# Output projections of a recurrent attention layer: one 512-column matmul per head instead of four of 128, with an fp32 fold

## The chip, the core and the metric

The kernel runs on one core of a Trainium2 chip. The core has a matrix engine (PE, with its weight loads shown apart as PEld), a vector engine (DVE), a scalar engine (ACT), a general engine (POOL) and a queue engine (SP); 16 DMA engines move data between the chip's memory (HBM) and the on-chip memory. Matmul results land in PSUM, of which a tile of 128 partitions by 512 fp32 numbers fills one bank of eight. The metric is the device time of one execution, in microseconds.

## The reference, cut to what matters

The program is a forward and backward pass of one block: a recurrent attention over segments of 32 rows with 8 memory rows, and a gated feed-forward layer. What the change touches is the recurrence:

```python
# S = 2048 rows, D = 512, H = 32 heads of 128, M = 8 memory rows, 64 segments of 32 rows
mem = mem0
for s in range(64):
    h = concatenate([mem, x[s]])                # 40 rows
    q, k, v = h@Wq, h@Wk, h@Wv                  # per head
    o = softmax(mask(q k^T * scale)) v          # per head, 40 rows
    o = einsum('bhte,hed->btd', o, Wo)          # output projection: sum over 32 heads
    mem = o[:, :8]                              # the next segment needs these 8 rows
    outs.append(o[:, 8:])
```

The backward pass runs the segments in reverse. There the gradient of `h` is a sum over 96 products (32 heads of dV, dK and dQ with the transposed Wv, Wk and Wq), and its 8 memory rows feed the segment before.

## The kernel before

`phase2` is the forward recurrence, `phase4` the backward one; `phase3` lies between them (the feed-forward layer, forward and backward), `phase5` behind (weight gradients). In `phase2` and `phase4` a segment is one turn of a Python loop over 64; everything is unrolled. The code is recorded in that order, and a scheduling layer then fixes each engine's own row of instructions; within an engine that row is kept at run time. Data of all heads lie as 12 groups of 128 columns, three heads of 40 rows to a group; `pi` counts three parts of four groups (12, 12 and 8 heads).

One forward segment: `proj_bank` makes Q, K and V (384 matmuls of 128x128 weights by 40 columns, line 371), then scores, exponentials, sums, products with V and transposes. `fillers` are transposes left over from the segment before, put into gaps. `outproj` (line 446) then takes 32 rows of every head as weights (a tile of 128x32) and multiplies with the head's 512 columns of `Wo`. `col_mms` (line 198) does that in four matmuls of 128 columns, one in each column tile of the array (`tile_position`), so that column chunk `c` of the sum over heads grows in partitions 32c to 32c+31 of `at_ps`. `rows_to_mem` (line 204) copies nothing but a transpose: `at_sb` (ACT, line 491), the transpose `memtp` (PE, line 208), and the copy of its 8 memory columns into the next segment's `hT` (DVE, line 209). `store_a` writes `at_sb` to the DRAM tensor `AOA`.

The remaining 8 rows of each head are collected by `TailRows` (POOL copies, line 1339) over four segments; their projection runs in four pieces (`chunk`, line 1363) into `ao_tps`, one piece per following segment, and ends with a DVE copy `ao_tsb` (line 1377).

The backward segment has the same end: `dot_bank` (128 matmuls of 40 columns, line 1004), transposes, `ds_part`, `grad_part` (dV, dK, dQ), and between them `dht` (line 1046), which calls `col_mms` 96 times into `dh_ps`; then `dh_sb` (line 1084), `memtp`, `dyT` (the next segment's input), and the tail pieces `dh_tps` of 24 heads each. The first matmul of the next segment reads `hT` or `dyT`, so a segment's end and the next one's beginning are a chain.

The lines before, word for word:

```python
        for c in range(self.cfg.DC):
            self.nc.tensor.matmul(ps[32 * c:32 * c + 32, :], lhsT=lhsT, rhs=w[:, c * 128:(c + 1) * 128],
                                  start=start, stop=stop, tile_position=(0, 32 * c))
```

Of the kernel before, what the change touches and what calls it, by code (L numbers as in the profile page):

```python
# [7 lines left out]
BF16 = mybir.dt.bfloat16  # L8
F32 = mybir.dt.float32
AF = mybir.ActivationFunctionType  # L10
# [30 lines left out]
class K:  # L41
# [73 lines left out]
    def phase0(self):  # L115
# [2 lines left out]
        D, DC = cfg.D, cfg.DC  # L118
        self.ident = const.tile([128, 128], BF16, name="ident")
        make_identity(nc, self.ident[:])  # L120
        self.ones = const.tile([128, 128], BF16, name="ones")
        nc.vector.memset(self.ones[:], 1.0)
        L, M = cfg.L, cfg.M
# [71 lines left out]
                nc.sync.dma_start(self.MODROW[:, q * 768:(q + 1) * 768],  # L195
                                  modrow[32 * q:32 * q + 1, :, :].rearrange("p h n -> p (h n)"))

    def col_mms(self, ps, lhsT, w, start, stop):

        for c in range(self.cfg.DC):  # L200
            self.nc.tensor.matmul(ps[32 * c:32 * c + 32, :], lhsT=lhsT, rhs=w[:, c * 128:(c + 1) * 128],  # L201
                                  start=start, stop=stop, tile_position=(0, 32 * c))

    def rows_to_mem(self, psp, rows_sb, dst):

        nc, M = self.nc, self.cfg.M
        tp = psp.tile([128, self.cfg.DC, 32], BF16, name="memtp", tag="p")
        nc.tensor.transpose(tp[:, :, :].rearrange("p c r -> p (c r)"), rows_sb[:], self.ident[:])  # L208
        nc.vector.tensor_copy(dst[:, :, 0:M], tp[:, :, 0:M])  # L209

    def load_x_rows(self, dst, j, a, b):

# [65 lines left out]
    def phase2(self):  # L278
# [6 lines left out]
        with ExitStack() as ctx:  # L285
# [42 lines left out]
            Qsts = ptiles("Qst", 2, zero=False)  # L328
            Ksts = ptiles("Kst", 2, zero=False)

            p1_tile = self.phase1_setup(ctx, lambda: ps_b16("p1tp"))
            P1_AHEAD = 3
# [57 lines left out]
                    fillers.pop(0)()  # L390

            nseg_t = 128 // T
            tail = TailRows(self, sb2, psb, 1, "ao", self.AOA, self.AOB)
            for s in range(NS):
                i2 = s % 2
                if s % nseg_t == 0:
# [48 lines left out]

                def outproj(pi):
                    if at_ps[0] is None:
                        at_ps[0] = psp.tile([128, 128], F32, name="at_ps", tag="p")
                    for h in range(pi * PG * 3, min(H, (pi + 1) * PG * 3)):
                        off = (h // 3) * GW + (h % 3) * L  # L450
                        self.col_mms(at_ps[0], OT[:, off:off + 32], Wo[:, h, :], n_at[0] == 0, n_at[0] == H - 1)
                        n_at[0] += 1

                proj_bank("q", 0, QT, hT, "act")
# [36 lines left out]
                nc.scalar.activation(at_sb[:], at_ps[0][:], AF.Copy)  # L491
                tail.collect(s % nseg_t, [OT])
                tail.chunk()
                if hT_next is not None:
                    self.rows_to_mem(psp, at_sb, hT_next)
                tail.store_a(s, at_sb)
                if s % nseg_t == nseg_t - 1:
                    tail.begin(s - nseg_t + 1, [Wo])
                nc.gpsimd.dma_start(self.VT[s], gl3(VT))
# [2 lines left out]
                    filler()  # L502

                def mk_fillers(s=s, i2=i2, QT=QT, KT=KT, ET=ET, rden=rden):
                    Pst, Qst, Kst = Psts[i2], Qsts[i2], Ksts[i2]
# [396 lines left out]
    def phase4(self):  # L902
# [7 lines left out]
        with self.p4_ctx as ctx:  # L910
# [69 lines left out]
            nc.vector.memset(dyT[:, :, 0:M], 0.0)  # L980
            get_loads(NS - 1)
            nseg_t = 128 // T
            tail = TailRows(self, sb2, psb, 3, "dh", self.DHA, self.DHB)
            for s in reversed(range(NS)):
                i2 = s % 2
                dyT = get_dy(s)
# [8 lines left out]
                dVT, dKT, dQT = dXTs["dVT"][i2], dXTs["dKT"][i2], dXTs["dQT"][i2]  # L995

                def dot_bank(hb, eng):
                    nh = 12 if hb < 2 else H - 24
# [46 lines left out]

                def dht(X, WT, pi):
                    if dh_ps[0] is None:
                        dh_ps[0] = psp.tile([128, 128], F32, name="dh_ps", tag="p")
                    for h in range(pi * PG * 3, min(H, (pi + 1) * PG * 3)):
                        off = (h // 3) * GW + (h % 3) * L  # L1050
                        self.col_mms(dh_ps[0], X[:, off:off + 32], WT[:, h, :], n_dh[0] == 0, n_dh[0] == 3 * H - 1)
                        n_dh[0] += 1

                dot_bank(0, "act")
# [25 lines left out]
                dht(dKT, WkT, 2)  # L1080
                for pi in range(NP):
                    dht(dQT, WqT, pi)
                dh_sb = sb2.tile([128, 128], BF16, name="dh_sb")
                nc.scalar.activation(dh_sb[:], dh_ps[0][:], AF.Copy)
                tail.collect(s % nseg_t, [dVT, dKT, dQT])
                tail.chunk()
                if dyT_next is not None:
                    self.rows_to_mem(psp, dh_sb, dyT_next)
                else:
                    dm = io["out_2"].rearrange("o m d -> (o m) d")  # L1090
                    for c in range(DC):
                        nc.sync.dma_start(dm[:, c * 128:(c + 1) * 128], dh_sb[32 * c:32 * c + M, :])
                tail.store_a(s, dh_sb)
# [228 lines left out]
class TailRows:  # L1322

    def __init__(self, k, pool, psb, n, name, dram_a, dram_b):
        self.k, self.pool, self.psb, self.n, self.name = k, pool, psb, n, name
        self.dram_a, self.dram_b = dram_a, dram_b
        self.cur = None
        self.pieces = []  # L1330

# [9 lines left out]
    def begin(self, s0, ws):  # L1341
        while self.pieces:
            self.chunk()
        cfg, H = self.k.cfg, self.k.cfg.H
        tiles, self.cur = self.cur, None
        order = [(i, h) for i in range(self.n) for h in range(H)]
        per = len(order) // 4
        st = {}

        def piece(u):  # L1350
            def f():
                if u == 0:
                    st["ps"] = self.psb.tile([128, 128], F32, name=f"{self.name}_tps")
                for n in range(u * per, (u + 1) * per):
                    i, h = order[n]
                    self.k.col_mms(st["ps"], tiles[i][:, h, :], ws[i][:, h, :], n == 0, n == len(order) - 1)
# [10 lines left out]
    def finish(self):  # L1367
        while self.pieces:
            self.chunk()

    def store_a(self, s, rows_sb):
        self.k.nc.gpsimd.dma_start(self.dram_a[s], rows_sb[:])

    def store_b(self, s0, ps):
        nc = self.k.nc
        b_sb = self.pool.tile([128, 128], BF16, name=f"{self.name}_tsb")
        nc.vector.tensor_copy(b_sb[:], ps[:])
        nc.gpsimd.dma_start(self.dram_b[s0 // 4], b_sb[:])


def build_kernel(tc, io, cfg, dbg=None):
# [82 lines left out]
```

## Time and profile before

| what | value |
|---|---|
| time, median of 3 runs | 4397.94 us (4396.47 to 4398.76) |
| the profiled execution's own time | 4405.3 us |
| its span, first to last instruction | 4403.5 us |
| busy share: PE, PEld, DVE, ACT, POOL | 84%, 67%, 43%, 35%, 17% |
| instructions shown | 205821, of these 96124 matmuls and 96124 weight loads |
| TensorE clock granted, mean | 0.945 of full speed |
| first and last `at_sb` (forward segments) | 109.6 and 1427.6 us |
| first and last `dh_sb` (backward segments) | 2089.4 and 3522.4 us |

How to read the rows. A timeline row has the start in us from the span's start, the duration in us (from the first start to the last end where `xN` rows are merged), engine, line, operation, out<-in, and in brackets the idle time of the engine before it with what ended it. "issue" there means that the engine waited for nothing the profile shows. A row of a group has the total busy time in us and the mean of one in ns behind the bar. In a row of waits stand the total in us, the count, and the longest. A row of windows has the length of a stretch, each engine's busy time with its instructions, the granted clock (1.00 is full speed), the share of the DMA engines, and GB/s.

### The profile page before, as it was taken

Reading aid. Unit: us, or ns where it says so; the run is one execution under the profiler, and the core shown is the slowest. Engines: PE = TensorE matmul, PEld = TensorE weight load, DVE = VectorE, ACT = ScalarE, POOL = GpSimd, SP = SyncE. Lnnn points to the kernel's source line nnn. Section 1 sums busy time; section 2 is a strip of 40 time slices with the busy share of each in tenths; the row PEclk is TensorE's granted clock in tenths of the full one; section 3 lists DMA queues with packets and bytes.
Section 4 is the critical chain, followed back from the end, with each engine's and each line's share of the span. In section 5 each row is a group of like instructions: output and inputs, shape, how many; then the busy total and the mean of one; then the engine's idle time right before and its main releaser. Section 6 shows DMA issues by size and latency. Waiting matters only on the chain. (4 is left out here: it accounts for less than half of the span.)

```text
span 4403.5 us, 205821 instructions
## 1 busy us (share of the span) xinstructions
PE 3700.6 (84%) x96124; PEld 2971.5 (67%) x96124; DVE 1878.4 (43%) x3840; ACT 1528.5 (35%) x2666; POOL 748.9 (17%) x1191
## 2 busy tenths in 40 slices
PE   2999999999999699798877877777778839999996
PEld 2888888888888455355766766677767726666653
DVE  3444444444444577422333332333333326655454
ACT  0333434343344454312222222222222225555553
POOL 2111111111111233211111111111111112111000
PEclk6999999999999899899999899999998969999998
DMA  6223333333222433377444444444444378777673
GB/s 217 103 101 104 108 111 102 103 108 105 97 106 105 163 118 115 124 228 226 150 150 150 141 139 142 150 149 136 143 144 150 113 143 185 163 157 161 144 155 108
DMA packets 559132, 607.61 MB, mean 138 GB/s; under 512 B 367082, under 2 KB 453370, under 8 KB 556612
## 3 DMA queue, kind: packets, MB, share of 16 engines
q1 hardware_dynamic: 489220, 316.00, 26.8%
q0 software_dynamic: 61200, 264.55, 17.4%
q8 instruction: 751, 12.30, 1.2%
q10 hardware_dynamic: 7856, 13.89, 1.0%
q14 instruction: 105, 0.86, 0.1%
HBM read 319.29 MB, written 275.02 MB: 135 GB/s over the span
## 5 line engine op out<-in xcount | busy, mean ns | idle before, releaser
L1232 PE MATMUL gps<-rows,hrows 128*128 128x384 bf16 (+1 forms) x2640 | 460.8, 322 | 11.3 <-ACT ot L61 8.9
L1232 PEld LDWEIGHTS <-hrows 128*128 128x128 bf16 x2640 | 253.2, 98 | 148.7 <-issue 13.9
L63 DVE COPY rows<-tpg 128x384 bf16<-128x384 bf16 (+1 forms) x616 | 199.6, 349 | 275.0 <-PE tpg L1225 147.1
L201 PE MATMUL dh_ps<-WqT,dQT 128*32 128x128 bf16 x8192 | 176.2, 252 | 148.1 <-issue 147.7
L1225 PE MATMUL tpg<-ident,xr 128*128 128x128 bf16 x2560 | 222.9, 221 | 83.0 <-ACT xr L1218 60.8
L1225 PEld LDWEIGHTS <-xr 128*128 128x128 bf16 x2560 | 181.4, 98 | 141.8 <-ACT xr L1218 60.9
L1004 PE MATMUL proj_ps<-dyT,WoT 128*128 128x40 bf16 x8192 | 242.7, 183 | 26.8 <-issue 23.6
L371 PE MATMUL proj_ps<-hT,Wq 128*128 128x40 bf16 x8192 | 243.0, 180 | 26.0 <-issue 16.3
L201 PEld LDWEIGHTS <-dQT 128*32 128x32 bf16 x8192 | 154.6, 114 | 159.6 <-issue 159.3
L1218 ACT ACTIVATE xr<-xt 128x3072 bf16<-128x3072 bf16 (+1 forms) x44 | 234.8, 5338 | 70.0 <-DMA x<-in_A_x_dram 68.9
L1004 PEld LDWEIGHTS <-WoT 128*128 128x128 bf16 x8192 | 231.7, 98 | 38.3 <-issue 33.6
L209 DVE COPY dyT<-memtp 128x32 bf16<-128x32 bf16 x63 | 10.9, 174 | 567.4 <-PE memtp L208 567.4
L371 PEld LDWEIGHTS <-Wq 128*128 128x128 bf16 x8192 | 227.7, 96 | 36.7 <-issue 32.9
L371 PE MATMUL proj_ps<-hT,Wk 128*128 128x40 bf16 x8192 | 242.3, 180 | 10.0 <-issue 9.7
L371 PE MATMUL proj_ps<-hT,Wv 128*128 128x40 bf16 x8192 | 235.1, 180 | 2.2 <-issue 1.0
L371 PEld LDWEIGHTS <-Wk 128*128 128x128 bf16 x8192 | 226.7, 96 | 13.4 <-issue 12.6
L371 PEld LDWEIGHTS <-Wv 128*128 128x128 bf16 x8192 | 224.6, 96 | 3.7 <-issue 3.5
L201 PE MATMUL dh_ps<-WkT,dKT 128*32 128x128 bf16 x8192 | 154.0, 222 | 80.1 <-issue 79.8
L61 ACT ACTIVATE dOT<-proj_ps 128x480 bf16<-128x480 f32 (+2 forms) x192 | 68.4, 391 | 433.7 <-PE proj_ps L1004 424.0
L63 DVE CAST KT<-proj_ps 128x480 bf16<-128x480 f32 (+2 forms) x256 | 119.6, 488 | 211.1 <-PE proj_ps L371 206.2
L61 ACT ACTIVATE QT<-proj_ps 128x480 bf16<-128x480 f32 (+2 forms) x256 | 104.9, 436 | 279.7 <-PE proj_ps L371 277.6
L1219 DVE COPY xr<-xt 128x4608 bf16<-128x4608 bf16 (+1 forms) x44 | 176.3, 4008 | 48.7 <-DMA dhb<-DHA 48.7
(306 smaller groups left out, 7813.6 us busy)
## 6 DMA issues: line engine op xcount, KB each, us to landing
VT<-VT POOLq DMA_DIRECT2D x64, 384.0 KB, 2.7
OT<-OT POOLq DMA_DIRECT2D x64, 384.0 KB, 3.7
PS<-Pst POOLq DMA_DIRECT2D x64, 384.0 KB, 3.2
QST<-Qst POOLq DMA_DIRECT2D x64, 384.0 KB, 3.3
KST<-Kst POOLq DMA_DIRECT2D x64, 384.0 KB, 4.1
OT_l<-OT SPq DMA_DIRECT2D x64, 384.0 KB
VT_l<-VT SPq DMA_DIRECT2D x64, 384.0 KB
Pst_l<-PS SPq DMA_DIRECT2D x64, 384.0 KB
```

What stands on the lines that cost most here:

```text
L61: return nc.scalar.activation(out, in_, AF.Copy)
L63: return nc.vector.tensor_copy(out, in_)
L201: self.nc.tensor.matmul(ps[32 * c:32 * c + 32, :], lhsT=lhsT, rhs=w[:, c * 128:(c + 1) * 128], start=start, stop=stop, tile_position=(0, 3 ...
L209: nc.vector.tensor_copy(dst[:, :, 0:M], tp[:, :, 0:M])
L371: nc.tensor.matmul(ps[:, g_, hl * L:(hl + 1) * L], lhsT=Ws[w][:, c, h * E:(h + 1) * E], rhs=hT[:, c, :], start=(c == 0), stop=(c == DC - 1))
L1004: nc.tensor.matmul(ps[:, g_, hl * L:(hl + 1) * L], lhsT=WoT[:, c, h * E:(h + 1) * E], rhs=dyT[:, c, :], start=(c == 0), stop=(c == DC - 1))
L1218: nc.scalar.activation(xr[:, 0:cut, :], xt[:, :, 0:cut].rearrange("p s x -> p x s"), AF.Copy)
L1219: nc.vector.tensor_copy(xr[:, cut:W, :], xt[:, :, cut:W].rearrange("p s x -> p x s"))
L1225: nc.tensor.transpose(ps[0:KR, hl, :], xr[:, c0:c0 + 2, :].rearrange("p a s -> p (a s)"), self.ident[:, :])
L1232: nc.tensor.matmul(ps[:, 0:nh * E], lhsT=hrows[0:KR, tp_, c * 128:(c + 1) * 128], rhs=rows[0:KR, tp_, 0:nh * E], start=(tp_ == 0), stop=(t ...
```

## The change

Each head's projection becomes one matmul of 512 columns. Head number `n` goes to column tile `n % 4`, so that each column tile sums every fourth head over all 512 columns, and `at_ps`, `dh_ps` and the tail sums become whole banks ([128, 512]). The four partial sums are then folded by `fold`: ACT and DVE copy half of the bank each to the fp32 tile `part`, and four fp32 matmuls with that copy as weights and a constant 128x32 selection matrix (`foldsel`, four stacked unit matrices) give the sum transposed, as [128, 4, 32]. From this ACT copies the 8 memory columns straight to the next segment's `hT` or `dyT`. `store_rows` makes the rows for DRAM (DVE cast, PE transpose, ACT copy, DMA). The tail's sum is folded and stored in the same way. To make room, four tiles are kept once instead of twice: `Qst`, `Kst`, `dKT` and `dQT`.

```diff
-    def col_mms(self, ps, lhsT, w, start, stop):
-        for c in range(self.cfg.DC):
-            self.nc.tensor.matmul(ps[32 * c:32 * c + 32, :], lhsT=lhsT, rhs=w[:, c * 128:(c + 1) * 128],
-                                  start=start, stop=stop, tile_position=(0, 32 * c))
-    def rows_to_mem(self, psp, rows_sb, dst):
-        nc, M = self.nc, self.cfg.M
-        tp = psp.tile([128, self.cfg.DC, 32], BF16, name="memtp", tag="p")
-        nc.tensor.transpose(tp[:, :, :].rearrange("p c r -> p (c r)"), rows_sb[:], self.ident[:])
-        nc.vector.tensor_copy(dst[:, :, 0:M], tp[:, :, 0:M])
+    def col_mm(self, ps, lhsT, w, n, total):
+        j = n % 4
+        self.nc.tensor.matmul(ps[32 * j:32 * j + 32, :], lhsT=lhsT, rhs=w, start=(n < 4), stop=(n >= total - 4),
+                              tile_position=(0, 32 * j))
+    def fold(self, psp, pool, ps, name, tag):
+        nc, DC = self.nc, self.cfg.DC
+        sb = pool.tile([128, 512], F32, name=name + "_part", tag="part")
+        nc.scalar.activation(sb[:, 0:256], ps[:, 0:256], AF.Copy)
+        nc.vector.tensor_copy(sb[:, 256:512], ps[:, 256:512])
+        ft = psp.tile([128, DC, 32], F32, name=name + "_ft", tag=tag)
+        for c in range(DC):
+            nc.tensor.matmul(ft[:, c, :], lhsT=sb[:, c * 128:(c + 1) * 128], rhs=self.foldsel[:], start=True, stop=True)
+        return ft
+    def store_rows(self, psp, pool, ft, dram, name, tag):
+        nc = self.nc
+        tb = pool.tile([128, 128], BF16, name=name + "_tb")
+        nc.vector.tensor_copy(tb[:], ft[:].rearrange("p c r -> p (c r)"))
+        tp = psp.tile([128, 128], BF16, name=name + "_tp", tag=tag)
+        nc.tensor.transpose(tp[:], tb[:], self.ident[:])
+        rb = pool.tile([128, 128], BF16, name=name + "_rb")
+        nc.scalar.activation(rb[:], tp[:], AF.Copy)
+        nc.gpsimd.dma_start(dram, rb[:])
+        return rb
...
-                at_sb = sb2.tile([128, 128], BF16, name="at_sb")
-                nc.scalar.activation(at_sb[:], at_ps[0][:], AF.Copy)
                 tail.collect(s % nseg_t, [OT])
                 tail.chunk()
+                ft = self.fold(psp, sb2, at_ps[0], "at", "p")
                 if hT_next is not None:
-                    self.rows_to_mem(psp, at_sb, hT_next)
-                tail.store_a(s, at_sb)
+                    nc.scalar.activation(hT_next[:, :, 0:M], ft[:, :, 0:M], AF.Copy)
+                self.store_rows(psp, sb2, ft, self.AOA[s], "at", "p")
...
-            dXTs = {nm: ptiles(nm, 2, zero=False) for nm in ("dVT", "dKT", "dQT")}
+            dXTs = {nm: ptiles(nm, n, zero=False) for nm, n in (("dVT", 2), ("dKT", 1), ("dQT", 1))}
...
                 if u == 3:
-                    self.store_b(s0, st["ps"])
+                    ft = self.k.fold(self.psp, self.pool, st["ps"], self.name + "_b", "p")
+                    self.k.store_rows(self.psp, self.pool, ft, self.dram_b[s0 // 4], self.name + "_b", "p")
```

The backward segment's end changes in the same way (`dh_ps`, `dyT`, `DHA`).

On PE, the row of a backward segment at the first `dht` call, before: one head of `dVT` (the weights) takes four pairs of weight load and matmul, of which two are shown.

```order
L1035 LDWEIGHTS dOst_54558
L1035 MATMUL g_ps<-Pst_l,dOst_54558 128x128
L201 LDWEIGHTS dVT_54559
L201 MATMUL dh_ps<-WvT,dVT_54559 32x128
L201 LDWEIGHTS dVT_54559
L201 MATMUL dh_ps<-WvT,dVT_54559 32x128
```

The same place after the change:

```order
L1056 LDWEIGHTS dOst_47715
L1056 MATMUL g_ps<-Pst_l,dOst_47715 128x128
L207 LDWEIGHTS dVT_47717
L207 MATMUL dh_ps<-WvT,dVT_47717 32x512
L207 LDWEIGHTS dVT_47717
L207 MATMUL dh_ps<-WvT,dVT_47717 32x512
```

The shapes tell the difference: a pair now does a whole head. PE's row as a whole goes from 192250 instructions to 131100.

On PE at the end of a backward segment, before (`dh_tps` is a tail piece, `memtp` the transpose of the segment's sum; behind the last 11 tail matmuls, of which two are shown, come those of the next segment's `dot_bank`):

```order
L201 LDWEIGHTS dh_tail_57909
L201 MATMUL dh_tps<-WkT,dh_tail_57909 32x128
L208 LDWEIGHTS dh_sb
L208 MATMUL memtp<-ident,dh_sb 128x128
L201 LDWEIGHTS dh_tail_57909
L201 MATMUL dh_tps<-WkT,dh_tail_57909 32x128
```

After, in two pieces: the fold matmuls, and the last rows of the segment.

```order
L207 LDWEIGHTS dh_tail_49661
L207 MATMUL dh_tps<-WvT,dh_tail_49661 32x512
L218 MATMUL dh_ft<-foldsel,dh_part 128x32 x2
L207 LDWEIGHTS dh_tail_49661
L207 MATMUL dh_tps<-WvT,dh_tail_49661 32x512
```

```order
L207 LDWEIGHTS dh_tail_49662
L207 MATMUL dh_tps<-WkT,dh_tail_49662 32x512
L227 LDWEIGHTS dh_tb
L227 MATMUL dh_tp<-ident,dh_tb 128x128
L1025 LDWEIGHTS WoT
L1025 MATMUL proj_ps<-dyT,WoT 128x40
```

The fold's fp32 matmuls have no weight load of their own in the row. Of a segment's 24 tail matmuls, here 8 stand ahead of the first two fold matmuls, 4 between these and the other two, and 12 behind; the transpose of the rows for DRAM stands ahead of the next segment's first matmul.

On PE at the end of a forward segment, before: `memtp` stands between two groups of 12 tail matmuls.

```order
L201 LDWEIGHTS ao_tail_12999
L201 MATMUL ao_tps<-Wo,ao_tail_12999 32x128
L208 LDWEIGHTS at_sb
L208 MATMUL memtp<-ident,at_sb 128x128
L201 LDWEIGHTS ao_tail_12999
```

After (`at_ft` is the fold, `at_tp` the transpose of the rows for DRAM):

```order
L207 LDWEIGHTS OT_492
L207 MATMUL at_ps<-Wo,OT_492 32x512
L218 MATMUL at_ft<-foldsel,at_part 128x32 x4
L227 LDWEIGHTS at_tb
L227 MATMUL at_tp<-ident,at_tb 128x128
```

Here the tail piece has moved to an earlier place in most segments, and no other matmul stands between the last projection and the next segment's first.

More of the change, by code (lines that the diff above doesn't have):

```diff
@@ L120, in phase0 @@
         make_identity(nc, self.ident[:])
+        self.foldsel = const.tile([128, 32], F32, name="foldsel")
+        fs2 = const.tile([128, 2, 32], F32, name="foldsel2")
+        for i in range(2):
+            nc.vector.tensor_tensor(fs2[:, i, :], self.ident[:, 64 * i:64 * i + 32], self.ident[:, 64 * i + 32:64 * i + 64],
+                                    op=ALU.add)
+        nc.vector.tensor_tensor(self.foldsel[:], fs2[:, 0, :], fs2[:, 1, :], op=ALU.add)
         self.ones = const.tile([128, 128], BF16, name="ones")
@@ L327, in phase2 @@
             Psts = ptiles("Pst", 2)
-            Qsts = ptiles("Qst", 2, zero=False)
-            Ksts = ptiles("Kst", 2, zero=False)
+            Qsts = ptiles("Qst", 1, zero=False)
+            Ksts = ptiles("Kst", 1, zero=False)
             p1_tile = self.phase1_setup(ctx, lambda: ps_b16("p1tp"))
@@ L392, in phase2 @@
             nseg_t = 128 // T
-            tail = TailRows(self, sb2, psb, 1, "ao", self.AOA, self.AOB)
+            tail = TailRows(self, sb2, psp, psb, 1, "ao", self.AOB)
             for s in range(NS):
@@ L447, in outproj @@
                     if at_ps[0] is None:
-                        at_ps[0] = psp.tile([128, 128], F32, name="at_ps", tag="p")
+                        at_ps[0] = psp.tile([128, 512], F32, name="at_ps", tag="p")
                     for h in range(pi * PG * 3, min(H, (pi + 1) * PG * 3)):
                         off = (h // 3) * GW + (h % 3) * L
-                        self.col_mms(at_ps[0], OT[:, off:off + 32], Wo[:, h, :], n_at[0] == 0, n_at[0] == H - 1)
+                        self.col_mm(at_ps[0], OT[:, off:off + 32], Wo[:, h, :], n_at[0], H)
                         n_at[0] += 1
@@ L504, in mk_fillers @@
                 def mk_fillers(s=s, i2=i2, QT=QT, KT=KT, ET=ET, rden=rden):
-                    Pst, Qst, Kst = Psts[i2], Qsts[i2], Ksts[i2]
+                    Pst, Qst, Kst = Psts[i2], Qsts[0], Ksts[0]
                     def f_x(src, dst, dram, pi, eng):
@@ L982, in phase4 @@
             nseg_t = 128 // T
-            tail = TailRows(self, sb2, psb, 3, "dh", self.DHA, self.DHB)
+            tail = TailRows(self, sb2, psp, psb, 3, "dh", self.DHB)
             for s in reversed(range(NS)):
@@ L994, in phase4 @@
                 dOT, prodO, dS, dST, dOst = dOTs[0], prodOs[0], dSs[0], dSTs[0], dOsts[0]
-                dVT, dKT, dQT = dXTs["dVT"][i2], dXTs["dKT"][i2], dXTs["dQT"][i2]
+                dVT, dKT, dQT = dXTs["dVT"][i2], dXTs["dKT"][0], dXTs["dQT"][0]
                 def dot_bank(hb, eng):
@@ L1047, in dht @@
                     if dh_ps[0] is None:
-                        dh_ps[0] = psp.tile([128, 128], F32, name="dh_ps", tag="p")
+                        dh_ps[0] = psp.tile([128, 512], F32, name="dh_ps", tag="p")
                     for h in range(pi * PG * 3, min(H, (pi + 1) * PG * 3)):
                         off = (h // 3) * GW + (h % 3) * L
-                        self.col_mms(dh_ps[0], X[:, off:off + 32], WT[:, h, :], n_dh[0] == 0, n_dh[0] == 3 * H - 1)
+                        self.col_mm(dh_ps[0], X[:, off:off + 32], WT[:, h, :], n_dh[0], 3 * H)
                         n_dh[0] += 1
@@ L1082, in phase4 @@
                     dht(dQT, WqT, pi)
-                dh_sb = sb2.tile([128, 128], BF16, name="dh_sb")
-                nc.scalar.activation(dh_sb[:], dh_ps[0][:], AF.Copy)
                 tail.collect(s % nseg_t, [dVT, dKT, dQT])
                 tail.chunk()
+                ft = self.fold(psp, sb2, dh_ps[0], "dh", "p")
                 if dyT_next is not None:
-                    self.rows_to_mem(psp, dh_sb, dyT_next)
-                else:
+                    nc.scalar.activation(dyT_next[:, :, 0:M], ft[:, :, 0:M], AF.Copy)
+                rb = self.store_rows(psp, sb2, ft, self.DHA[s], "dh", "p")
+                if s == 0:
                     dm = io["out_2"].rearrange("o m d -> (o m) d")
                     for c in range(DC):
-                        nc.sync.dma_start(dm[:, c * 128:(c + 1) * 128], dh_sb[32 * c:32 * c + M, :])
-                tail.store_a(s, dh_sb)
+                        nc.sync.dma_start(dm[:, c * 128:(c + 1) * 128], rb[32 * c:32 * c + M, :])
                 if s % nseg_t == 0:
@@ L1352, in f @@
                 if u == 0:
-                    st["ps"] = self.psb.tile([128, 128], F32, name=f"{self.name}_tps")
+                    st["ps"] = self.psb.tile([128, 512], F32, name=f"{self.name}_tps", tag="b")
                 for n in range(u * per, (u + 1) * per):
                     i, h = order[n]
-                    self.k.col_mms(st["ps"], tiles[i][:, h, :], ws[i][:, h, :], n == 0, n == len(order) - 1)
+                    self.k.col_mm(st["ps"], tiles[i][:, h, :], ws[i][:, h, :], n, len(order))
                 if u == 3:
-                    self.store_b(s0, st["ps"])
+                    ft = self.k.fold(self.psp, self.pool, st["ps"], self.name + "_b", "p")
+                    self.k.store_rows(self.psp, self.pool, ft, self.dram_b[s0 // 4], self.name + "_b", "p")
             return f
```

13 lines of the change are left out of this document (3 added, 10 removed).

## The prediction

> **What bounds the kernel now.** I read the page first: PE is busy for 84% of the span, so the end is set by PE's row of matmuls and by what that row waits for. Then PE's waits, then two stretches of equal kind of work (forward, backward), then PE's timeline in the backward stage. The page, and a DMA queue that carries instructions:
>
> ```profile
> span 4403.5 us, 205821 instructions
> PE 3700.6 (84%) x96124; PEld 2971.5 (67%) x96124; DVE 1878.4 (43%) x3840; ACT 1528.5 (35%) x2666; POOL 748.9 (17%) x1191
> ...
> q8 instruction: 751, 12.30, 1.2%
> ```
>
> PE's waits by line, and two windows (forward first, backward second):
>
> ```profile
> PE dh_ps L201 <- issue: 233.2, 122, 4.5
> ...
> PE dh_tps L201 <- issue: 46.8, 42, 2.0
> ...
> PE proj_ps L371 <- issue: 27.0, 64, 1.1
> PE proj_ps L1004 <- issue: 23.6, 28, 1.3
> ...
> PE ao_tps L201 <- issue: 4.4, 7, 1.3
> ...
> PE at_ps L201 <- issue: 2.9, 7, 0.7
> ```
>
> ```profile
> 200.00:400.00 200.00, 186.43 (x6229) 172.03 (x6225) 91.18 (x193) 79.24 (x175) 36.24 (x70) 1.00 0.30 104
> 2700.00:3000.00 300.00, 236.63 (x9083) 212.39 (x9086) 99.99 (x225) 64.07 (x130) 44.38 (x95) 0.92 0.44 144
> ```
>
> The largest wait of PE is for nothing that the profile names: 280 us in the backward projections and their tails. The timeline shows what it is:
>
> ```profile
> 2101.33 0.52 PE L201 MATMUL dh_ps<-WvT,dVT 128*32 128x128 bf16 x23 [0.70 <-issue]
> 2101.78 0.40 PE L1035 MATMUL g_ps<-dST,Kst_l 128*128 128x128 bf16 x4
> 2102.11 0.85 PE L201 MATMUL dh_ps<-WkT,dKT 128*32 128x128 bf16 x48
> 2102.89 0.40 PE L1035 MATMUL g_ps<-dST,Kst_l 128*128 128x128 bf16 x4
> 2103.22 0.90 PE L201 MATMUL dh_ps<-WkT,dKT 128*32 128x128 bf16 x49
> 2106.45 0.37 PE L201 MATMUL dh_ps<-WkT,dKT 128*32 128x128 bf16 x12 [2.33 <-issue]
> ```
>
> Between the two stalls lie 23+4+48+4+49 = 128 matmuls, with their weight loads 256 instructions. PE's row has 192250 instructions, and 192250/256 = 751, the packet count of the instruction queue (12.30 MB/751 = 16 KB each). So PE runs out of instructions at the edge of a 256-instruction page. It uses them up fastest in these lines: 48 matmuls in 0.85 us, less the 0.22 us that one takes, are 13.4 ns each, a page in 1.7 us. How much a segment loses:
>
> ```profile
> L491 ACT ACTIVATE at_sb<-at_ps x64: 277/277/278, 109.6 to 1427.6; 128x128 bf16<-128x128 f32 x64
> ```
>
> ```profile
> L1084 ACT ACTIVATE dh_sb<-dh_ps x64: 277/277/278, 2089.4 to 3522.4; 128x128 bf16<-128x128 f32 x64
> ```
>
> ```profile
> 2111.47 2.56 PE L1004 MATMUL proj_ps<-dyT,WoT 128*128 128x40 bf16 x96 [0.27 <-DVE dyT L209]
> ...
> 2121.71 0.41 PE L201 MATMUL dh_ps<-WkT,dKT 128*32 128x128 bf16 x16
> ```
>
> A backward segment takes (3522.4-2089.4)/63 = 22.75 us, a forward one (1427.6-109.6)/63 = 20.92. Without stalls a backward one would take 10.24 us (2111.47 to 2121.71, none in it), 0.78 for 12 heads of dKT and 0.33 for `g_ps` (2102.11 to 2103.22), 208 matmuls at 13.4 ns = 2.79, a tail piece of 96 = 1.29, and some 0.35 for `memtp`: 15.8 us. So 6.95 us of each of the 64 are lost, 445 us; 304 of them are the stalls of lines 201 and 1004, and the other 141 go with the clock, 0.92 against 1.00 forward, where PE hardly stalls.
>
> **The change, part by part.**
>
> *Streaming: nothing.* A head costs PE 4 x 13.4 = 53.6 ns before, since four column tiles run side by side. Four heads of 512 columns side by side take four times that. That long streams overlap too is shown by the only wide column-tile matmuls of the trace:
>
> ```profile
> 21.13 0.33 PE L190 MATMUL modrow_ps<-wmod,sclo_bc 128*32 128x384 bf16 x4
> ...
> 21.29 0.33 PE L190 MATMUL modrow_ps<-wmod,schi_bc 128*32 128x384 bf16 x4
> ```
>
> Groups of four with 384 columns start 0.16 us apart, which is 4 x 13.4 x 3 = 0.16: full overlap, weight loads hidden.
>
> *Instructions: the gain.* PE's row falls to 131100. A backward segment had 256 instructions of `dot_bank`, 168 around 84 matmuls of 128 columns, 768 of `dht`, 192 of tail and 2: 1386, or 5.41 pages, one per 4.2 us. Now it has 256+168+192+48+6 = 670, 2.6 pages, 11 us of fetching at that pace in a segment of some 17. I take all 445 us as won. Forward, the stalls above are 27.0+4.4+2.9 = 34 us; 1308 instructions become about 1080. Won: 34.
>
> [...]
>
> *The fold: the cost.* Rows for its pieces:
>
> ```profile
> L63 DVE CAST KT<-proj_ps 128x240 bf16<-128x240 f32 x64 | 26.0, 407 | 7.3 <-PE proj_ps L371 2.4
> ...
> L1004 PEld LDWEIGHTS <-WoT 128*128 128x128 bf16 x8192 | 231.7, 98 | 38.3 <-issue 33.6
> ...
> L421 PE MATMUL dc_ps<-ones,ET 128*128 128x1 bf16 x768 | 46.2, 164 | 0.3 <-issue 0.3
> ```
>
> ```profile
> L1377 DVE CAST ao_tsb<-ao_tps x16: 278/282/292, 212.2 to 1432.6; 128x128 bf16<-128x128 f32 x16
> ```
>
> The copies of 256 columns take about 0.42 us on DVE (240 take 0.407), ACT's lie beside them. The `tb` cast is 0.28. The fp32 matmul is nowhere in the trace. Its lower bound is the 25 ns at which the 40-column matmuls follow each other (2.40 us for 96): 0.10 us for four. [...] I take 1.05 us for four. In PE's row these matmuls have no weight load of their own, so the load cannot run ahead, and one load and one matmul in series are 0.26 us. [...] Half and double of it are well possible.
>
> [...]
>
> Backward: from the last `dQT` stream's end PE has 8 tail matmuls (0.43 us) while the copies need 0.22 (the matmul's own length) + 0.42 + 0.05, so it waits about 0.25; the fold 1.05; five changes between column tiles and the whole array at 0.14 (0.78 for 48 matmuls that stream in 0.64) 0.70; `dh_tp` 0.06. The 12 tail matmuls behind cover cast and ACT's copy into `dyT`. That is 2.05 against 0.35 for `memtp`: +1.7, 109 us over 64. A tail fold every fourth segment: 16 x (1.05+0.75) = 29.
>
> Forward there is no cover:
>
> ```profile
> 529.67 1.30 PE L201 MATMUL at_ps<-Wo,OT 128*32 128x128 bf16 x80
> ...
> 531.07 0.28 ACT L491 ACTIVATE at_sb<-at_ps 128x128 bf16<-128x128 f32 x1 [0.64 <-PE at_ps L201]
> ...
> 531.40 0.23 PE L208 MATMUL memtp<-ident,at_sb 128*128 128x128 bf16 x1 [0.27 <-ACT at_sb L491]
> ...
> 531.67 0.17 DVE L209 COPY hT<-memtp 128x32 bf16<-128x32 bf16 x1 [3.96 <-PE memtp L208]
> ...
> 531.90 0.60 PE L371 MATMUL proj_ps<-hT,Wq 128*128 128x40 bf16 x18
> ```
>
> The stream ends at 529.67+80 x 0.0134 = 530.74, the next segment starts 1.16 us later. Now: 0.22+0.05, copies 0.42+0.05, fold 1.05, then 0.05, cast 0.28, 0.05, and `at_tp` with its load 0.13: 2.3. The Q projection stands behind `at_tp` in PE's row and so waits for the cast too; ACT's copy to `hT` runs beside it. +1.15, 74 us over 64; tail folds 16 x 1.5 = 24.
>
> *At nothing:* the single copies of `dKT`, `dQT`, `Qst`, `Kst`. A store must have left before the next segment writes:
>
> ```profile
> DKT<-dKT POOLq DMA_DIRECT2D x64, 384.0 KB, 5.9
> ```
>
> ```profile
> 2804.67 0.54 POOL L1097 DMA_DIRECT2D DKT<-dKT  x1
> ...
> 2822.36 0.39 PE L1035 MATMUL g_ps<-dS,Qst_l 128*128 128x128 bf16 x4
> ```
>
> `dKT` has left at 2810.6, and is written again from 2822.4; with segments 5 us shorter 6 us remain. If these went, DVE's copy out of `g_ps`, and PE behind its PSUM, would wait that long. Removed `at_sb` and `memtp` copies and the added `rb` copies on ACT lie beside PE's matmuls; POOL's number of DMAs stays.
>
> **The sum.** Backward -445+109+29 = -307; forward -34+74+24 = +64; in all -243. The profiled execution took 4405.3 us, 7.4 above the median; 4398-243 = 4155 us against the median, -5.5%.
>
> **The rivals.**
>
> [...]
>
> [...]
>
> *Column tiles with other weights in each, and 512 columns, don't overlap their loads:* a round of four then waits for about 98+3 x 13.4 = 138 ns. 30 rounds backward and 10 forward a segment, 64 x 40 x 0.138 = +353: 4508, slower. The 0.16 us of line 190 speaks against it. [...]
>
> *Fetching stays the bound.* With segments of 17.5 us the DMA engines' share rises from 0.44 to 0.44 x 22.75/17.5 = 0.57; if a page then took 8 us instead of 4.2, a backward segment would last 2.6 x 8 = 21 us: +3.5 x 64 = 224, 4379, still faster. From 6.7 us a page on it matters.
>
> *The fold is cheap:* 0.4 us instead of 1.05 gives 4051; it is in the range's low end.
>
> **How the numbers follow.** The likeliest, fold 0.6 to 1.7 us and stalls gone (4083 to 4259): 0.66. Fold below that: 0.08. Fold 1.7 to 2.5 (4259 to 4387): 0.10. Fetching still the bound: 0.04. Fold above 2.57: 0.06; loads not overlapped 0.03; fetching not the cause 0.03. Faster 0.66+0.08+0.10+0.04 = 0.88, minus what lies near the point where it turns: 0.86; same (within 0.2%, 9 us, about what a measurement of this kernel tells from no change) 0.02; slower 0.12. The range: fold from 0.5 to 2.0 us, 4067 to 4307.
>
> **What would show it.** Right: `dh_ps` waits for "issue" under 40 us in all instead of 233, the granted clock in the backward window at 0.97 or more, `dh_sb`'s successor `dh_part` every 17 to 18 us, `part` every 22 forward, the instruction queue at 131100/256 = 512 packets. The fp32 rows `at_ft` give the fold's price directly. Wrong: `at_ft` groups of over 2.5 us, rounds of `dh_ps` over 0.3 us apart, or stalls still 256 instructions apart.

## The result, and the profile after

The changed kernel takes 4126.6 us (median of 4 runs, 4120.61 to 4126.9) beside 4397.99 (4396.47 to 4398.76): a ratio of 0.938, 95% interval 0.9364 to 0.9396. The forecast was 4155, range 4067 to 4307.

The page of the changed kernel:

```profile
span 4125.1 us, 147177 instructions
...
PE 3714.4 (90%) x66669; PEld 2687.0 (65%) x66718; DVE 1960.2 (48%) x4005; ACT 1619.0 (39%) x2984; POOL 749.7 (18%) x1191
...
q8 instruction: 521, 8.54, 0.9%
```

PE's waits by line, the two longest of those in the recurrences; the list has no "issue" entry left for the projections, the tails or `proj_ps`:

```profile
PE at_tp L227 <- DVE at_tb L225: 29.5, 48, 0.6
PE at_ft L218 <- ACT at_part L214: 23.4, 48, 0.5
```

The backward window, and the first copy of each segment's sum (its first and last start give the stages' lengths, as `at_sb` and `dh_sb` did before):

```profile
2150.00:3200.00 1050.00, 1038.58 (x20577) 715.01 (x20574) 499.82 (x1114) 339.32 (x750) 201.74 (x434) 0.99 0.56 187
```

```profile
L214 ACT ACTIVATE at_part<-at_ps x64: 383/383/385, 108.6 to 1481.5; 128x256 f32<-128x256 f32 x64
```

```profile
L214 ACT ACTIVATE dh_part<-dh_ps x64: 378/383/383, 2140.9 to 3240.7; 128x256 f32<-128x256 f32 x64
```

Between the first and the last sum the forward stage went from 1318.0 us to 1372.9 (a segment from 20.92 to 21.79), the backward stage from 1433.0 to 1099.8 (22.75 to 17.46). So, in the two profiled executions (4405.3 and 4126.9 us), the forward recurrence lost 55 us, the backward one won 333, and each other stretch of the program is the same within 4 us. The granted clock backward is 0.99 instead of 0.92.

### The profile page after: what moved, and what is told of

It is laid out like the page before. It is cut to its first block, busy times and chain, and to the rows that moved or that the text cites. A ratio compares the mean times of both kernels' runs of the same rounds, so it can differ in the third digit from the quotient of the medians.

```text
span 4125.1 us, 147177 instructions
## 1 busy us (share of the span) xinstructions
PE 3714.4 (90%) x66669; PEld 2687.0 (65%) x66718; DVE 1960.2 (48%) x4005; ACT 1619.0 (39%) x2984; POOL 749.7 (18%) x1191
## 5 line engine op out<-in xcount | busy, mean ns | idle before, releaser
L1025 PE MATMUL proj_ps<-dyT,WoT 128*128 128x40 bf16 x8192 | 228.4, 180 | 2.3 <-DMA dyT<-DAOT 2.3
L1025 PEld LDWEIGHTS <-WoT 128*128 128x128 bf16 x8192 | 221.8, 96 | 2.8 <-issue 2.8
L438 ACT ACTIVATE ET<-st_ps 128x480 bf16<-128x480 f32 x192 | 109.5, 570 | 226.9 <-PE st_ps L437 226.8
L61 ACT ACTIVATE rows<-tpg 128x384 bf16<-128x384 bf16 (+1 forms) x264 | 126.7, 480 | 159.2 <-PE tpg L1245 159.1
L539 DVE TENSOR_TENSOR Pst<-tps,rden 120x512 bf16<-120x512 bf16 x192 | 131.5, 686 | 100.0 <-PE tps L405 100.0
L61 ACT ACTIVATE dVT<-g_ps 128x512 bf16<-128x512 f32 x192 | 114.6, 597 | 135.7 <-PE g_ps L1056 135.7
L61 ACT ACTIVATE dQT<-g_ps 128x512 bf16<-128x512 f32 x192 | 114.6, 597 | 113.4 <-PE g_ps L1056 113.4
```

What stands on the lines that cost most here:

```text
L61: return nc.scalar.activation(out, in_, AF.Copy)
L438: nc.scalar.activation(part3(ET, pi)[:, :, 0:120], st_ps[:, :, 0:120], AF.Exp, scale=cfg.scale)
L1025: nc.tensor.matmul(ps[:, g_, hl * L:(hl + 1) * L], lhsT=WoT[:, c, h * E:(h + 1) * E], rhs=dyT[:, c, :], start=(c == 0), stop=(c == DC - 1))
```

## The experiments

They ran in three groups, on the chips numbered 8 and 15, each group beside the kernel before, which takes 4364 to 4366 us there. The control run below, the changed kernel again, stands in the group of chip 15 (4118 us, ratio 0.9436, 0.942 to 0.9451). So each run is read by its ratio to the kernel before of its own group, against 0.9436, and by its own profile; differences in us from the control are between chips for the runs of chip 8.

### Is it the number of instructions?

The changed kernel with its sums and its fold, but four matmuls per head again, all in the head's own column tile:

```diff
-        self.nc.tensor.matmul(ps[32 * j:32 * j + 32, :], lhsT=lhsT, rhs=w, ...)
+        # the heads of four column tiles together (pend), then
+        for c in range(4):
+            for j, (l, wj) in enumerate(pend):
+                self.nc.tensor.matmul(ps[32 * j:32 * j + 32, c * 128:(c + 1) * 128], lhsT=l,
+                                      rhs=wj[:, c * 128:(c + 1) * 128], ...)
```

> The changed kernel with its sums and its fold kept, but each head's 512 columns cut into four matmuls of 128 columns in the head's own column tile, so that PE's row has 192510 instructions again instead of 131100. Theory (instruction fetching was the loss): the stalls come back 256 instructions apart, 'issue' waits in the backward projections of 200 us or more, granted clock there near 0.92, a backward segment of 22 to 25 us instead of 17.5, and about 4127 + 445 + 34 = 4606 us, at least 4500. Rival (the gain comes from the layout, from sums per tile and longer streams, and not from the count): 4127 within 40 us, no more 'issue' waits than the changed kernel has.

Measured: 4550.39 us, ratio 1.0426 (1.039 to 1.0463), 432 us more than the control: above the 4500, below the 4606 that I had expected. PE's waits by line:

```profile
PE dh_ps L214 <- issue: 220.6, 124, 4.8
...
PE dh_tps L214 <- issue: 35.7, 36, 2.0
```

A window inside its backward stage (PE, PEld, DVE, ACT, POOL, then the granted clock, the DMA share and GB/s):

```profile
2200.00:3600.00 1400.00, 1139.22 (x41409) 1026.35 (x41410) 492.67 (x1097) 334.02 (x740) 198.52 (x427) 0.92 0.42 140
```

The waits have their old places too. Two of them, one after the other:

```profile
2421.26 0.52 PE L214 MATMUL dh_ps<-WkT,dKT 128*32 128x128 bf16 x24 [2.64 <-issue]
2421.61 2.31 PE L214 MATMUL dh_ps<-WqT,dQT 128*32 128x128 bf16 x104
2424.73 0.51 PE L214 MATMUL dh_ps<-WqT,dQT 128*32 128x128 bf16 x12 [0.82 <-issue]
```

Between the two lie 24+104 = 128 matmuls, 256 instructions with their loads. In that window the trace has 119 gaps of over 0.8 us between the starts of PE's instructions, and 116 of the 118 distances between them are multiples of 256 instructions, to within two.

Each head still goes to its own column tile, with the sums, the fold and the tails of the changed kernel; the count came back, and with it the waits, the clock of 0.92 and the loss. A backward segment takes 23.62 us, a forward one 22.18, so that 391 of the 432 us lie in the backward stage and 26 in the forward one. The rival, which puts the gain down to the layout, is out; streams of 128 columns came back with the count, but stalls 256 instructions apart speak for the count. How much of the 391 us beyond the named waits (256 us in these two lines) is due to the clock was not measured apart.

### Does each instruction cost, or only too many of them?

Two matmuls of 256 columns per head, so a third of the instructions taken out are back:

```diff
+        for c in range(2):
+            j = 2 * (n % 2) + c
+            self.nc.tensor.matmul(ps[32 * j:32 * j + 32, :], lhsT=lhsT, rhs=w[:, c * 256:(c + 1) * 256], start=(n < 2),
+                                  stop=(n >= total - 2), tile_position=(0, 32 * j))
```

> Two matmuls of 256 columns per head (even heads in column tiles 0 and 1, odd heads in 2 and 3), two partial sums per column half instead of four, a PSUM sum of 256 columns, and the fold with copies of 128 columns each and the same number of fp32 matmuls. PE's row has 151520 instructions: a third of the instructions taken out are back. Theory (a threshold: what counts is whether a segment's pages arrive within the segment): 914 instructions per backward segment are 3.6 pages, 15 us at 4.2 us a page, under 17.4, so no stalls come back; the copies are 0.1 us shorter: ratio 0.932 to 0.940, 'issue' waits in the backward projections below 20 us. Rival (each instruction costs its share, in fetching or in issue): a third of the 479 us comes back, +160 us, ratio 0.974.

Measured: 4129.4 us, 0.9457 (0.9431 to 0.9483): no difference in the whole from the changed kernel that these intervals show, and far from the 0.974 of a cost per instruction. The ratio misses the expected 0.932 to 0.940, as does the control's own 0.9436. The whole hides two parts: a forward segment takes 21.64 us (control 21.76), a backward one 17.90 (17.42), so the backward stage is 30 us longer and the forward one 8 shorter. A few stalls are back, 19 us in all:

```profile
PE dh_tps L206 <- issue: 13.1, 15, 2.2
...
PE dh_ps L206 <- issue: 3.2, 2, 2.0
PE proj_ps L1025 <- issue: 2.7, 2, 1.4
```

So there is a threshold, though not a sharp one: 3.6 pages of 256 instructions in a segment of 17.9 us still come almost in time, 5.4 do not. A third of the instructions brought back 30 us in the backward stage, where a third of the 391 us above would be 130. What makes up the 11 us beyond the stalls was not taken apart. The forward stage before the change lies at the edge as well: 1308 instructions are 5.1 pages in 20.92 us, 4.1 us a page, with 34 us of such waits in all.

### What sets the time of a page?

The kernel before the change, with its backward loads done once:

```diff
+                if loads:
+                    return next(iter(loads.values()))
                 if s not in loads:
```

> The kernel before the change, with the five loads per backward segment (OT, VT, P, Q, K: 1.9 MB) done once for the first segment and its tiles used for all 64, which leaves out the other segments' data; PE's row is the same, 192250 instructions. Question: what sets the 4.2 us per page of instructions. Theory A (the pages queue behind data on the DMA engines): with the share of the DMA engines falling from 0.44 to some 0.15, a page takes the 3.4 us of the fastest tenth before; 5.41 pages are 18.7 us, a backward segment 18.7 to 20.5 instead of 22.75, 144 to 259 us less: ratio 0.940 to 0.967. Theory B (the 4.2 us are the round trip of one fetch at a time, whatever else moves): a segment stays at 22 to 23 us, ratio 0.99 to 1.00.

Measured: 4235.03 us, ratio 0.9705 (0.9688 to 0.9722), between the two, just outside theory A's range. The stage's window and its segments:

```profile
2100.00:3300.00 1200.00, 989.47 (x40582) 890.40 (x40580) 448.33 (x1010) 289.23 (x587) 199.08 (x427) 0.98 0.19 66
```

```profile
L1086 ACT ACTIVATE dh_sb<-dh_ps x64: 277/278/278, 2072.7 to 3356.5; 128x128 bf16<-128x128 f32 x64
```

A segment takes (3356.5-2072.7)/63 = 20.38 us, which is 3.77 us for each of its 5.41 pages, against 4.2 with the loads (a mean over the segment: PE does not wait at every page's edge). The 4.2 are from the first comparison's chip; beside the kernel before of its own group this run is 129 us shorter, 2.0 us a segment, which would put the segment with loads at 22.4 us there, 4.14 a page. With the DMA share at 0.19 instead of 0.44 the fetching is some 10% quicker, and PE still waits:

```profile
PE dh_ps L201 <- issue: 125.1, 82, 2.6
PE dh_tps L201 <- issue: 73.1, 47, 2.1
```

The packets of the instruction queue (q8, 16 KB each) show the pace directly: 330 of them in the 1400 us from 2100 us on before, one per 4.24 us, 317 in the 1200 us of the window here, one per 3.79. The quickest tenth of their starts lie 3.4 us apart in both (3.41 and 3.45), and a packet itself takes 1.1 us in both; it is the long distances that went (slowest tenth from 5.5 us on before, from 4.3 here).

So both theories hold a part. Taking the loads away made a page some 0.4 us quicker; most of the 4.2 us is there without them, and what fills the 3.4 us no run here shows. No wait of PE for one of the five loads stands in the list of either kernel, so, as far as PE's waits show, their removal moved the end through the instruction queue. The granted clock rose with it, from 0.92 to 0.98, and this run doesn't part the two.

### What is the fold worth, and which part of its chain?

The fold in bf16:

```diff
-        sb = pool.tile([128, 512], F32, name=name + "_part", tag="part")
+        sb = pool.tile([128, 512], BF16, name=name + "_part", tag="part")
...
-        self.foldsel = const.tile([128, 32], F32, name="foldsel")
+        self.foldsel = const.tile([128, 32], BF16, name="foldsel")
```

> The changed kernel with the partial sums copied as bf16 and the selection matrix in bf16, so that a fold is four bf16 matmuls (the rounding of the four partial sums is what differs). Theory (the fold lies on the chain between segments in both recurrences, 0.9 us each in fp32): four matmuls at 56 ns take 0.22, 0.67 us less on 128 folds and on some of the 32 tail folds: 86 to 107 us less, 4020 to 4041 us. Rival (the fold is beside other work and something else is late next, such as the copies): less than 30 us gained, above 4097.

Measured: 4018.04 us, 0.9213 (0.9185 to 0.9241), 100 us below the control. Both stages gained: a forward segment 21.09 us (control 21.76), a backward one 16.66 (17.42). The fold lies on the chain in both, as the theory has it; the rival is out.

ACT alone copies:

```diff
-        nc.scalar.activation(sb[:, 0:256], ps[:, 0:256], AF.Copy)
-        nc.vector.tensor_copy(sb[:, 256:512], ps[:, 256:512])
+        nc.scalar.activation(sb[:], ps[:], AF.Copy)
```

> The changed kernel with ACT alone copying all 512 columns of the sum, instead of 256 by ACT and 256 by DVE. Theory (the two halves do not run beside each other: in the changed kernel's timeline DVE's half starts when ACT's has ended, 0.38 + 0.04 + 0.42 = 0.85 us): one copy of 512 columns takes 0.60 us, so a chain is 0.25 us shorter on 128 folds, 32 us, and up to 8 us for the tails: 4087 to 4100 us. Rival (the halves overlap and only look serial through DVE's semaphore): 0.60 instead of 0.42 us, 4126.6 + 0.18 x 128 = 4150 us.

Measured: 4122.92 us, 0.9449 (0.9423 to 0.9475): no gain; the theory fell. The rival did not hold either, since the halves do run one after the other. The changed kernel's timeline at the end of a forward segment shows why the order is harmless (rows of a tail fold between them left out):

```profile
502.38 1.26 PE L207 MATMUL at_ps<-Wo,OT 128*32 128x512 bf16 x20
503.69 0.38 ACT L214 ACTIVATE at_part<-at_ps 128x256 f32<-128x256 f32 x1 [0.37 <-PE at_ps L207]
...
504.11 0.42 DVE L215 COPY at_part<-at_ps 128x256 f32<-128x256 f32 x1 [3.43 <-ACT at_part L214]
504.13 1.09 PE L218 MATMUL at_ft<-foldsel,at_part 128*128 128x32 f32 x8 [0.49 <-ACT at_part L214]
...
505.26 0.20 ACT L516 ACTIVATE hT<-at_ft 128x32 bf16<-128x32 f32 x1 [0.91 <-PE at_ft L218]
505.49 0.29 DVE L225 CAST at_tb<-at_ft 128x128 bf16<-128x128 f32 x1 [0.62 <-ACT hT L516]
505.83 0.23 PE L227 MATMUL at_tp<-ident,at_tb 128*128 128x128 bf16 x1 [0.61 <-DVE at_tb L225]
505.90 1.36 PE L393 MATMUL proj_ps<-hT,Wq 128*128 128x40 bf16 x48
```

DVE's copy starts when ACT's has ended, but PE starts folding at 504.13, when ACT's half alone is there, and DVE's half (until 504.53) is ready when the first two of the four fp32 matmuls are through. Two halves in series are a pipeline with the fold; one copy of 0.60 us delays the fold's start by 0.22. The segments agree: with ACT alone a forward segment takes 21.96 us (control 21.76), a backward one 17.40 (17.42).

The rows for DRAM behind the next segment's first bank (the calls of `store_rows` are kept and made after `proj_bank("q", 0, ...)` and `dot_bank(0, ...)`):

```diff
-                self.store_rows(psp, sb2, ft, self.AOA[s], "at", "p")
+                late.append(lambda ft=ft, s=s: self.store_rows(psp, sb2, ft, self.AOA[s], "at", "p"))
...
                 proj_bank("q", 0, QT, hT, "act")
+                if late:
+                    late.pop()()
```

> The changed kernel with the rows for DRAM (cast, transpose, copy, store) put behind the next segment's first bank of matmuls, so that the first bank waits for ACT's copy of the memory columns alone. Theory (in the changed kernel DVE's cast waits for ACT's copy, and the first bank stands behind the transpose that waits for the cast; 0.35 to 0.45 us a forward segment; backward 12 tail matmuls cover it): 22 to 29 us less, ratio 0.931 to 0.933. Rival (the first bank has to wait for ACT's copy as long): within 6 us, 0.937 to 0.939.

Measured: 4080.1 us, 0.9351 (0.933 to 0.9372), 38 us below the control, where 22 to 29 were expected; the ratio lies above the expected 0.931 to 0.933, as the control's lies above 0.938. In its timeline the first bank waits for `hT` and no longer for `at_tp`:

```profile
545.51 0.20 ACT L519 ACTIVATE hT<-at_ft 128x32 bf16<-128x32 f32 x1 [1.18 <-PE at_ft L218]
545.74 0.29 DVE L225 CAST at_tb<-at_ft 128x128 bf16<-128x128 f32 x1 [0.95 <-ACT hT L519]
545.76 1.35 PE L393 MATMUL proj_ps<-hT,Wq 128*128 128x40 bf16 x48 [0.28 <-ACT hT L519]
546.97 0.22 PE L227 MATMUL at_tp<-ident,at_tb 128*128 128x128 bf16 x1
```

The forward segment fell by 0.29 us (21.76 to 21.47), a little less than expected; the backward one by 0.26 (17.42 to 17.16), where I had expected nothing because 12 tail matmuls cover the cast. The backward ends of the changed kernel (first three rows) and of this one (last two) show where to look:

```profile
2613.96 0.20 ACT L1108 ACTIVATE dyT<-dh_ft 128x32 bf16<-128x32 f32 x1 [0.59 <-PE dh_ft L218]
...
2614.61 0.23 PE L227 MATMUL dh_tp<-ident,dh_tb 128*128 128x128 bf16 x1
...
2614.68 2.56 PE L1025 MATMUL proj_ps<-dyT,WoT 128*128 128x40 bf16 x96
```

```profile
2600.81 0.20 ACT L1116 ACTIVATE dyT<-dh_ft 128x32 bf16<-128x32 f32 x1 [1.47 <-PE dh_ft L218]
...
2601.06 1.35 PE L1031 MATMUL proj_ps<-dyT,WoT 128*128 128x40 bf16 x48
```

In the changed kernel the next segment's first bank starts 0.52 us after ACT's copy to `dyT` has ended (2614.16 to 2614.68), behind tail matmuls, cast and transpose; here it starts 0.05 us after (2601.01 to 2601.06). But the scheduling layer also put most of this segment's tail matmuls ahead of the fold, and the share of each was not taken apart.

### One half of the change, and the control

The changed kernel again:

> The changed kernel once more, so that the others of this call stand beside it on one chip. All theories: ratio to the kernel before 0.936 to 0.940, a forward segment 21.8 us, a backward one 17.4 to 17.5.

Measured: 4118.32 us, 0.9436; forward 21.76, backward 17.42 us a segment. The segments are those of the first comparison, within 0.04 us. The ratio is not, because the kernel before is 32 us faster here.

The backward recurrence changed, the forward one as before:

> The backward recurrence as changed, the forward one as before (four matmuls of 128 columns, one transpose). Theory (each recurrence stands by itself; forward the fold's chain of 2.4 us costs more than the stalls it removes): the 54 us that the forward stage grew come back, 4126.6 - 54 = 4072 us, range 4060 to 4085, ratio 0.926. Rival (the forward stage gains from fewer instructions too, and its growth is paid by something else, such as the single copies of Qst and Kst): 4110 or more.

Measured: 4043.32 us, 0.9263 (0.9244 to 0.9283), 75 us below the control. The ratio is as expected (0.926); the time lies below the expected 4060 to 4085, which had been taken from the first comparison. The forward stage fell from 1371.0 to 1306.4 us, 65 of the 75. The forward half of the change, as it stands, is a loss. This run also keeps `Qst` and `Kst` twice again, so by itself it doesn't tell the fold's chain from the rival of the single copies.

The two gains together, first without and then with late rows:

> The backward recurrence as changed but with the bf16 fold, the forward one as before. Theory (the two gains stand side by side): the bf16 fold took 50 us out of the backward stage in the run before (1099.8 to 1049.5), the forward stage as before takes out 54 to 66: ratio 0.9263 - 50/4398 = 0.915, range 0.912 to 0.918. Rival (the fold's saving came in the forward stage alone): 0.926.

Measured: 3986.03 us, 0.9129 (0.9112 to 0.9146), as the theory has it.

> The forward recurrence as before the change, the backward one changed with the bf16 fold and the late rows. Theory: the run without the late rows gave 0.9129, and late rows took 16 us out of the backward stage (1097.3 to 1080.9): 0.909, range 0.907 to 0.912; the fastest of all. Rival (with the forward stage of the other kernel of this call at 20.8 us a segment too, both are the same): within 0.003 of that kernel.

Measured: 3969.25 us, 0.9095 (0.9079 to 0.911), the lowest median of all. With the forward recurrence changed as well:

> The changed kernel with both the bf16 fold and the rows for DRAM put behind the next segment's first bank. Theory (the two shorten different links of the chain): 4118 - 97 - 38 = 3983 us beside that run's 4366, ratio 0.912, range 0.909 to 0.916; a forward segment 20.8 us. Rival (with the fold short, the copies of the sum or ACT's row become the last link, so that the second gain shrinks): 0.917 to 0.921.

Measured: 3980.31 us, 0.9125 (0.9101 to 0.9148). The two gains add up as the theory has it. A forward segment is 20.77 us in both of these kernels: with the fold short and the rows late, the changed forward end is just as good as the old one, and whether 3969 and 3980 differ lies within their intervals, so that the rival of the run before stands beside its theory. The second of these kernels keeps `Qst` and `Kst` once, the first twice: that their forward segments are equal speaks against a price of the single copies, though a loss there could be offset by a gain.

## Why the prediction was right, point by point

**The stalls.** Right. The 304 us of "issue" in lines 201 and 1004 are gone and the clock is at 0.99; putting the instructions back brought them back, and 432 us with them, against the chance of 0.03 that fetching is not the cause. That 141 of the 445 us go with the clock was not tested apart; in the run without the loads the clock is 0.98 with 198 of the 280 us of waits still there. The queue's packets came to 521 instead of 512: each fp32 matmul shows as two loads and two matmuls, 640 x 3 more instructions than I had counted, 7.5 of the 9 pages.

**Streaming.** Right. 32 matmuls of 512 columns follow each other as those of 128 did:

```profile
2608.45 1.90 PE L207 MATMUL dh_ps<-WqT,dQT 128*32 128x512 bf16 x32
```

Eight rounds of four, less the 0.38 us that one takes, are (1.90-0.38)/7 = 0.217 us a round, against 4 x 53.6 ns = 0.214. Loads of other weights into the four tiles cost nothing beyond those 0.003 us a round, so the rival of loads that don't overlap is out.

**The fold's price.** 1.05 us was taken, 0.92 was measured, in the profile of the changed kernel (this row, and the `at_ft` row of the timeline above):

```profile
L218 PE MATMUL at_ft<-foldsel,at_part x512: 248/276/297, 109.0 to 1484.2; 128*128 128x32 f32 x171
```

Eight records for four matmuls take 1.09 us with the first one's own 0.28, so they follow at some 0.115 us, and eight are 0.92. The 2.57 us among the chances, a fold's length from which on the change would have lost, are 1.05+243/160, for the 160 folds of the program; no run shows a fold that long. The size was close, the grounds less so: one load and one matmul in series for each product is not what happens, since the trace shows two loads and two matmuls for each, which follow at 0.115 us although a load by itself takes 0.19 and a matmul 0.28. One fp32 matmul is thus about 0.23 us. What each of its two records computes no run here shows.

**The forward chain.** 2.3 us was predicted, 503.45 (502.38 + 20 x 0.0536) to 505.90 is 2.45 in that segment, which has a tail fold in it. The stage's +55 us stands against +64. If the other segments are like this one, the chain cost some 10 us more than predicted, so the remaining terms, the stalls won and the tail folds, came out some 19 better; that part of the small miss is luck.

**The backward stage.** -333 against -307, the largest miss. The end of an ordinary segment, without a tail fold, shows which term was too large:

```profile
2628.77 0.60 PE L207 MATMUL dh_tps<-WvT,dh_tail 128*32 128x512 bf16 x8
2629.43 0.63 PE L218 MATMUL dh_ft<-foldsel,dh_part 128*128 128x32 f32 x4
2630.00 0.40 PE L207 MATMUL dh_tps<-WvT,dh_tail 128*32 128x512 bf16 x4
2630.33 0.63 PE L218 MATMUL dh_ft<-foldsel,dh_part 128*128 128x32 f32 x4
...
2631.65 0.23 PE L227 MATMUL dh_tp<-ident,dh_tb 128*128 128x128 bf16 x1
2631.72 2.56 PE L1025 MATMUL proj_ps<-dyT,WoT 128*128 128x40 bf16 x96
```

The eight tail matmuls ahead of the fold are through at 2628.77 + 8 x 0.054 = 2629.20, and the next segment's first bank starts 2.52 us later. The prediction's terms for this stretch are 0.25+1.05+0.70+0.06 and 16 tail matmuls at 0.054, 2.93 us. The 0.41 us between them are 26 us over 64 segments, if the others are like this one: 0.13 of it is the fold, the other 0.28 the waits and the changes of tile, which at 0.14 each were priced too high.

**The copies** beside each other: wrong, they run in series (ACT's 0.38 us, then DVE's 0.42), without harm, as the run with ACT alone shows. Why they don't overlap no run here shows.

**The single copies** at nothing: right as far as the waits show. No wait of ACT or DVE for the stores of `Qst`, `Kst` or `dKT` stands among the changed kernel's; one entry for `dQT`'s, of ACT's copy `dh_rb`, is 2.2 us in all.

**Fetching still the bound:** not so at 0.56 of the DMA engines, with one packet of the instruction queue per 6.5 us (161 in the 1050 us of the window above); the run with 256 columns, one per 5.0 us, shows that the edge is not far.

## What to carry to other kernels

Where the matrix engine waits for nothing that the profile names, look at how many instructions lie between the waits. Here they were 256 apart, and the wait was a shortage of instructions. Count the instructions per turn of the loop, divide by the 256 of a page, and compare with the turn's length: here 5.4 pages in an estimated 15.8 us of work stalled, 3.6 in 17.9 hardly. Where the count lies well below, there is little left to win by merging matmuls (here a ratio of 0.9457 at 3.6 pages and 0.9436 at 2.6), so look at each stage by itself: the same edit won 333 us in one recurrence and lost 55 in the other. What is bought with a longer chain at a turn's end (here a fold, a cast and a transpose) can be shortened afterwards, by putting what only the store to DRAM needs behind the next turn's first work (38 us here).

## What the runs showed of the hardware

- PE's instructions come in pages of 256, at one per 4.2 us in the backward stage at a DMA share of 0.44, and 3.8 us at 0.19, the quickest tenth 3.4 us apart in both. With 5.4 pages for an estimated 15.8 us of work the segment is held to the pages' pace (22.75 and 20.38 us).
- An fp32 matmul with 128x128 weights and 32 columns is two loads and two matmuls in the trace, and costs about 0.23 us, more than the bf16 one: with the bf16 fold a forward segment is 0.67 us shorter and a backward one 0.76.
- Four column tiles with different weights and 512 columns each run fully side by side (0.217 us a round).
- The kernel before took 4398 us beside the result and 4364 to 4366 us on chips 8 and 15, 0.7% less; the changed one 4127 us and, on chip 15, 4118, 0.2% less. Why, no run shows.
